# Keys of batches five to eight transposed by VectorE and DMA instead of TensorE, in a pooled-attention and expert kernel

## The chip, the core and the metric

The kernel runs on one core of one Trainium2 chip. A core has TensorE (PE, the matrix engine; its weight loads are listed as PEld), VectorE (DVE), ScalarE (ACT), GpSimd (POOL), the sync engine (SP), whose queue issues nearly all DMAs here, and 16 DMA engines. The metric is device time in microseconds (us) of one execution. Three executions of the kernel before gave 905.93, 906.12 and 907.04 us; the median is 906.12 us.

## What is computed

Two steps follow each other. The first is attention against pooled keys and values, for 8 batches, 8 heads, 576 positions and a head size of 64. The second is an expert layer with a sine in it, on 4608 tokens.

```python
k_p = k.reshape(B, H, Sp, pool, D).mean(axis=3)      # pool = 8, Sp = 72
v_p = v.reshape(B, H, Sp, pool, D).mean(axis=3)
scores = scale * np.matmul(q, k_p.transpose(0, 1, 3, 2))
scores = scores - np.max(scores, axis=-1, keepdims=True)
attn = np.exp(scores)
attn = attn / (np.sum(attn, axis=-1, keepdims=True) + 1e-09)
x = np.matmul(attn, v_p)                  # then (4608, 512)
h = x @ w_in
s = np.sin(alpha * h)
g = h + s * s / (alpha + 1e-09)
out = g @ w_out
```

Everything is float32. Of each head there are 72 pooled keys, each a sum over 8 neighbouring positions (the division by 8 is folded into the scale of the exponential).

## The kernel before

The work is written out by hand, in an order that each engine keeps: an instruction that waits holds up all that come behind it on its engine. The first expert product runs in nine units of 512 tokens. A unit has 28 slots, 4 groups (`J`) of 7 (`k`); in a slot TensorE does one product of the expert layer (`product`, line 837, four matmuls at line 845, each of them two records in the trace). The products follow a Strassen scheme, so VectorE and ScalarE form sums and copies between them. `carry(u)` (line 1175) puts the other work into the slots of unit u: `at(slot, f, ...)` appends f to the work of a slot. In units 1 to 6 this is the attention of batch b = u + 1, hidden beside the products, and the preparation of batch b + 1. (Batches are counted from 0 in the code, so "five to eight" are 4 to 7.) After the ninth unit, from about 430 us on, the second expert product runs; the change does not touch it.

The way of the keys of one batch:

- `load_k` (line 116) loads half of the heads in one DMA on SP's queue, 576 KB into the tile `kvin` (two buffers, shared with the values). A partition holds 24 consecutive positions, that is 3 pooled keys, of one head; 4 heads of 24 such rows make 96 partitions, head by head.
- `pool_rows` (line 127) adds the 8 positions on POOL, in three additions (line 131), the last of which writes half of the tile `kp` of 96 x (3 keys x 128). There is one buffer of `kp`.
- `k_t` (line 273) turns `kp` with three TensorE transposes (line 278) into a PSUM bank, and VectorE copies the bank to `kblk` (line 279), 64 rows of one half of the heads over 64 of the other, the 72 keys of a head in their natural order. There are two tiles `kblk`, for even and odd batches.
- `two_scores` (line 303) multiplies the turned queries, as weights, with the 72 key columns of each head (line 317): 72 matmuls of 64 x 64 x 72 per batch, in two blocks, each 72 columns side by side in a PSUM bank. `shifts` (line 328) subtracts the maximum on VectorE, and `exp`, `norm`, `turn` and `move` follow: `turn` (line 495) transposes in blocks of 32 x 32 on VectorE, `move` (line 514) puts the blocks to their places with 16 DMAs on SP's queue (line 521). `all_values` (line 600) ends the batch.

In unit u with 0 < u < 7, before the change: `sums_of_x` (line 806, VectorE, line 814) for products 7 and 4 in slot 0; scores in slots 3 and 5; `load_v` in slot 6; `load_q` of batch u + 2 in slot 7; `load_k` of batch b + 1 and its pooling in slot 12; `move` in slot 14; the queries of batch u + 2 are turned on VectorE and moved by 16 DMAs (`turn_q`, line 215, DMAs at line 243) in slots 23 to 25; `all_values` in slot 25; `k_t` of batch b + 1 in slot 26. In slot 2 VectorE also finishes the last group of the unit before (`finish`, line 1051, additions at line 1052), which frees a PSUM bank that the scores of slot 3 write. `store_g` (line 1063, DMAs at line 1066) stores a group's result.

Of the kernel before, what the change touches and what calls it, by code (L numbers as in the profile page):

```python
# [13 lines left out]
F32 = mybir.dt.float32  # L14
# [6 lines left out]
POOL = 8  # L21
# [19 lines left out]
class Kernel:  # L41
# [74 lines left out]
    def load_k(self, b, e):  # L116

        Sp, D, NP = self.Sp, self.D, self.NP
        m = Sp // 3
        t = self.kvp.tile([P, 2048], F32, name="kvin")[:NP * m, 0:3 * POOL * D]  # L120
        self.nc.sync.dma_start(out=t, in_=self.k[b, NP * e:NP * e + NP].rearrange("h (p x) d -> (h p) (x d)", x=3 * POOL))
# [136 lines left out]
    def attention(self, b):  # L258
# [14 lines left out]
        def k_t():  # L273
# [5 lines left out]
            nc.vector.tensor_copy(out=kb[:].rearrange("p hp (x j) -> p j hp x", j=3), in_=ps.rearrange("p j (hp x) -> p j hp x", hp=NP))  # L279

        def q_t(i, copy=nc.scalar.copy):

            n = rows[i]
# [19 lines left out]
        def two_scores(j):  # L303
# [3 lines left out]
            for i, banks in ((2 * j, (x, 7)), (2 * j + 1, (5, 6))):  # L307
# [3 lines left out]
                for t in (i, 4) if i == 3 else (i,):  # L311
                    for hp in range(NP):
                        r0, h = (64 * (hp // 2), NP + hp % 2) if t == 4 else (0, hp)
                        for r, q in columns(hp, t):
                            for e in range(2):
                                s = slice(64 * e, 64 * e + 64)
                                nc.tensor.matmul(ps[e][r0 + r:r0 + r + q.shape[-1], h, :], q[s], kb[s, hp, :], start=True, stop=True)  # L317
            for i, m, ps in tiles:
# [281 lines left out]
        def all_values():  # L600
# [30 lines left out]
        return SimpleNamespace(**{f.__name__: f for f in (k_t, q_t, products, score, two_scores, two_shifts, exp, norm, new_a, turn, move, values, values_rest, all_values,  # L631
                                                          k_head, k_last, q_head, rest_q, products_head, soft_shift, soft_exp, norm_head, norm_rest, a_head, a_rest)})
# [542 lines left out]
    def carry(self, u):  # L1175
# [57 lines left out]
        if 0 < u < last:  # L1233
# [367 lines left out]
```

## Time and profile before

| | |
|---|---|
| median of three runs | 906.12 us |
| profiled execution, device time | 903.92 us |
| its span, first to last instruction | 902.1 us |
| PE busy | 894.4 us (99%) |
| DVE busy | 679.4 us (75%) |
| ACT busy | 448.6 us (50%) |
| POOL busy | 212.2 us (24%) |
| granted TensorE clock | 1.00 |
| one unit of 1 to 5 (for instance 195 to 250 us) | 55 us: DVE busy 37.8, ACT 41.1, POOL 25.5; DMA engines 0.71 of the time |

The span is the time from the first to the last instruction of the profiled execution; some 1.8 us more lie around it. TensorE is busy nearly always, so a change in time has to appear as work that TensorE no longer does, or does more slowly, or as a wait in front of it. In a row of the timeline stand start, length, engine, line and operation of a run of like instructions, and in brackets how long the engine was idle before it and what ended that. The rows of one engine can overlap a little, since consecutive instructions are pipelined.

### The profile page before, as it was taken

What the parts mean: (1) busy time and instruction counts of PE and PEld (TensorE: products, weight loads), DVE (VectorE), ACT (ScalarE), POOL (GpSimd) and SP (SyncE); (2) the same over time, 40 slices, a digit from 0 to 9 for tenths busy, and PEclk for the clock granted to TensorE, in tenths of its full rate; (3) what the DMA queues carried; (4) which work ended last, traced back from release to release, by engine and by line L of the source; (5) the groups of instructions that cost most, each with busy time, mean ns of one, the idle gap of its engine ahead of it and who ended that gap; (6) DMA issues with size and microseconds to landing.
All of it is one profiled execution on the core that took longest, in us unless ns stands there. A gap on an engine that the chain in (4) does not pass through costs nothing.

```text
span 902.1 us, 17919 instructions
## 1 busy us (share of the span) xinstructions
PE 894.4 (99%) x7002; PEld 815.4 (90%) x7002; DVE 679.4 (75%) x1012; ACT 448.6 (50%) x1072; POOL 212.2 (24%) x216
## 2 busy tenths in 40 slices
PE   9999999999999999999999999999999999999998
PEld 5787888888888888888888999999999999999997
DVE  7685867768577675764558799979798888889895
ACT  5686776877768777687976611211111111111111
POOL 5797452824337252430000000000000000000000
PEclk9999999999999999999999999999999999999999
DMA  9955857759486595658226346261618162533401
GB/s 260 249 182 171 232 154 203 190 167 260 136 215 185 181 225 145 173 148 292 93 75 224 101 144 198 59 195 37 224 28 230 33 196 68 172 92 125 139 14 40
DMA packets 128746, 141.12 MB, mean 156 GB/s; under 512 B 46920, under 2 KB 95704, under 8 KB 128664
## 3 DMA queue, kind: packets, MB, share of 16 engines
q1 hardware_dynamic: 125880, 137.88, 53.4%
q10 hardware_dynamic: 2784, 2.11, 0.9%
q8 instruction: 55, 0.90, 0.5%
q14 instruction: 27, 0.22, 0.1%
HBM read 75.37 MB, written 47.19 MB: 136 GB/s over the span
## 4 chain that ended last, share of the span: by engine, by line
PE 96%; DVE 2%; ACT 1%; issue 0%; ACTq 0%; DVEq 0%
PE PS L845 44%; PE PS L1334 41%; PE PS L1030 3%; PE PS L317 2%; PE PS L610 2%; PE PS L623 1%; DVE x L1289 1%; PE PS L1098 0%; DVE s L1289 0%; ACT s L1007 0%; PE PS L422 0%; DVE h L1052 0%; DVE r L1289 0%; PE PS L568 0%; PE PS L289 0%; PE PS L278 0%
## 5 line engine op out<-in xcount | busy, mean ns | idle before, releaser
L845 PE MATMUL PS<-home,a 128*128 128x256 f32 x1104 | 258.0, 381 | 0.7 <-DVE h L819 0.6
L845 PEld LDWEIGHTS PS<-home,a 128*128 128x128 f32 x1104 | 205.3, 190 | 33.1 <-issue 4.5
L845 PE MATMUL PS<-home,as 128*128 128x256 f32 x768 | 182.7, 382 | 0.0
L845 PEld LDWEIGHTS PS<-home,as 128*128 128x128 f32 x768 | 141.8, 190 | 19.7 <-ACT PS L820 1.2
L1384 POOL TENSOR_TENSOR cc<-cc,cb 128x576 f32<-128x576 f32 x1 | 2.0, 1978 | 501.6 <-DVE cb L1289 501.6
L1334 PE MATMUL PS<-s,wb 128*128 128x144 f32 x896 | 119.1, 286 | 0.0
L1334 PEld LDWEIGHTS PS<-s,wb 128*128 128x128 f32 x896 | 113.7, 190 | 0.1
L1007 ACT ACTIVATE s<-s,c 128x256 f32<-128x256 f32 (+1 forms) x228 | 113.5, 565 | 0.0
L819 DVE TENSOR_TENSOR h<-PS,p 128x512 f32<-128x512 f32 x72 | 49.1, 683 | 62.9 <-PE PS L845 37.3
L131 POOL TENSOR_TENSOR kvin<-kvin 96x768 f32<-96x768 f32 (+3 forms) x42 | 74.2, 1768 | 72.2 <-DMA kvin<-in_v_dram 70.0
L1462 ACT COPY PS<-PS 128x144 f32<-128x144 f32 x56 | 14.7, 263 | 144.8 <-PE PS L1334 140.7
L1000 ACT ACTIVATE s<-h,al 128x256 f32<-128x256 f32 x144 | 65.6, 509 | 37.3 <-DVE h L819 37.3
L1334 PE MATMUL PS<-r,wb 128*128 128x144 f32 x512 | 73.3, 286 | 0.3 <-DVE r L1289 0.3
L1334 PE MATMUL PS<-s,a 128*128 128x144 f32 x512 | 73.2, 286 | 0.0
L1000 ACT ACTIVATE s<-PS,al 128x256 f32<-128x256 f32 x144 | 60.0, 469 | 20.2 <-PE PS L845 19.2
L1052 DVE TENSOR_TENSOR h<-PS,s 128x512 f32<-128x512 f32 x36 | 24.7, 686 | 58.5 <-ACT s L1007 58.5
L1334 PEld LDWEIGHTS PS<-r,wb 128*128 128x128 f32 x512 | 67.1, 190 | 0.5 <-DVE r L1289 0.5
L1334 PEld LDWEIGHTS PS<-s,a 128*128 128x128 f32 x512 | 67.0, 190 | 0.0
L820 ACT COPY PS<-PS 128x512 f32<-128x512 f32 x72 | 41.5, 576 | 35.6 <-PE PS L845 30.8
L1482 ACT COPY PS<-PS 128x144 f32<-128x144 f32 x56 | 14.7, 263 | 88.1 <-PE PS L1334 88.1
L1052 DVE TENSOR_TENSOR h<-h,s 128x1024 f32<-128x1024 f32 x36 | 55.3, 1537 | 0.9 <-ACT s L1007 0.9
L1334 PE MATMUL PS<-s,we 128*128 128x144 f32 x384 | 54.9, 286 | 0.0
(216 smaller groups left out, 1407.6 us busy)
## 6 DMA issues: line engine op xcount, KB each, us to landing
g_bridge<-h SPq DMA_DIRECT2D x72, 512.0 KB
r<-g_bridge SPq DMA_DIRECT2D x31, 1152.0 KB
out_dram<-o SPq DMA_DIRECT2D x122, 72.0 KB
kvin<-in_k_dram SPq DMA_DIRECT2D x14, 576.0 KB
q<-in_q_dram SPq DMA_DIRECT2D x7, 1024.0 KB
kvin<-in_v_dram SPq DMA_DIRECT2D x14, 512.0 KB
aM<-tr SPq DMA_DIRECT2D x54, 92.0 KB
aM<-tr SPq DMA_DIRECT2D x54, 88.0 KB
```

The lines of the kernel that those rows point to most:

```text
L131: self.nc.gpsimd.tensor_tensor(out=t[..., 0:w] if w > D else out, in0=t[..., 0:w], in1=t[..., w:2 * w], op=OP.add)
L317: nc.tensor.matmul(ps[e][r0 + r:r0 + r + q.shape[-1], h, :], q[s], kb[s, hp, :], start=True, stop=True)
L610: nc.tensor.matmul(o[r:r + 64], w, x, start=start and i < 2, stop=False, skip_group_check=True)
L819: add = lambda o, x, y: nc.vector.tensor_tensor(out=o, in0=x, in1=y, op=OP.add)
L820: copy = lambda o, x: nc.scalar.copy(out=o, in_=x)
L845: nc.tensor.matmul(ps[:, jj, :], self.A[p][:, kk, f * P:(f + 1) * P], x[:, kk, :], start=(start and n == 0), stop=(kk == 1), skip_group_ch ...
L1000: self.nc.scalar.activation(out=G.s[:, i, jj, j, :], in_=src[:, jj], func=AF.Sin, scale=self.al[:, f:f + 1])
L1007: self.nc.scalar.activation(out=x, in_=x, func=AF.Square, scale=self.c[:, f:f + 1])
L1030: nc.tensor.matmul(o, W[m][:, G.J - J0], X[m], start=start and n == 0, stop=True, skip_group_check=True)
L1052: add = lambda o, x, y: self.nc.vector.tensor_tensor(out=o, in0=x, in1=y, op=OP.add)
L1334: nc.tensor.matmul(out, W[:, J // 2, J % 2, :], A[:, J, :], start=(start and J == 0), stop=(J == self.NJ - 1), skip_group_check=True)
L1462: nc.scalar.copy(out=x1[:, 0, :], in_=x0[:, 1, :])
```

## The change

For batches 4 to 7 the keys are turned another way. The rows of `load_k` stand in another order: the 4 heads of the same 24 positions next to each other (partition = 4 x group + head). `k_turn` transposes `kp` (96 x 384) in blocks of 32 x 32 in one VectorE instruction into a new tile `k_tr`. `k_move` then copies 12 pieces of 32 partitions x 96 elements (384 bytes per partition, contiguous on both sides) from `k_tr` into `kblk` with 12 DMAs on SP's queue. The keys of a head then lie in `kblk` in three runs of 24, in an order in which the third of a key's index comes first; the score matmuls read these three runs and write each result column to the natural place of its key, so that within a run neighbouring columns are written in steps of three elements (12 bytes) of PSUM. The softmax behind it sees the same layout as before.

The places: the keys of batch 4 are loaded in slot 22 and pooled in slot 27 of unit 1, those of batches 5, 6 and 7 in slot 12 of units 2, 3 and 4 (before: in slot 12 of the units 2, 3, 4 and 5 for batches 4 to 7). `k_turn` stands in slot 0, behind the two `sums_of_x`, and `k_move` in slot 8, of the unit before the batch's own (units 2 to 5). `k_t` in slot 26 is left in units 0 and 1 only. Batches 1 to 3 go the old way.

```diff
 load_k:
-        self.nc.sync.dma_start(out=t, in_=self.k[b, NP * e:NP * e + NP].rearrange("h (p x) d -> (h p) (x d)", x=3 * POOL))
+        src = self.k[b, NP * e:NP * e + NP].rearrange("h (p x) d -> h p (x d)", x=3 * POOL)
+        self.nc.sync.dma_start(out=t, in_=src.rearrange("h p x -> (h p) x" if b < 4 else "h p x -> p h x"))
 attention:
+        def k_turn():
+            kp = self.kp.pop(b)
+            self.k_tr = self.ap.tile([NP * Sp // 3, 4 * NP * Sp // 3], F32, name="k_tr")[:]
+            nc.vector.transpose(out=self.k_tr.rearrange("p (c h j x) -> p j c x h", c=4, h=NP, j=3),
+                                in_=kp[:].rearrange("p j e d -> p j (e d)").rearrange("p j (c x h) -> p j c x h", c=4, h=NP))
+        def k_move():
+            n = NP * Sp // 3
+            for c in range(4):
+                for a in range(3):
+                    nc.sync.dma_start(out=kb[32 * c:32 * c + 32].rearrange("p h x -> p (h x)")[:, n * a:n * a + n],
+                                      in_=self.k_tr[32 * a:32 * a + 32, n * c:n * c + n])
+        def keys(hp, s, out):
+            if b < 4:
+                return out, kb[s, hp, :]
+            w = Sp // 3
+            k = kb[s].rearrange("p h x -> p (h x)").rearrange("p (a n) -> p a n", a=3)[:, :, w * hp:w * hp + w]
+            return out.rearrange("p (a x j) -> p a j x", a=3, j=3), k.rearrange("p a (j x) -> p a j x", j=3)
 two_scores:
-                                nc.tensor.matmul(ps[e][r0 + r:r0 + r + q.shape[-1], h, :], q[s], kb[s, hp, :], start=True, stop=True)
+                                out, k = keys(hp, s, ps[e][r0 + r:r0 + r + q.shape[-1], h, :])
+                                nc.tensor.matmul(out, q[s], k, start=True, stop=True)
 carry:
             for i in range(2):
-                if b < last:
-                    at(12, self.load_k, b + 1, i)
+                ahead = b + 1 + (u > 1)
+                if ahead <= last:
+                    at(12, self.load_k, ahead, i)
                     at(12, lambda i=i: self.pool_k[i]())
+                if u == 1:
+                    at(22, self.load_k, b + 2, i)
+                    at(27, lambda i=i: self.pool_k[i]())
             at(25, A.all_values)
-            if b < last:
+            if u == 1:
                 at(26, self.att[b + 1].k_t)
+            elif b < last:
+                at(0, self.att[b + 1].k_turn)
+                at(8, self.att[b + 1].k_move)
```

More of the change, by code (lines that the diff above doesn't have):

```diff
@@ L629, in all_values @@
             to_x(rest, slice(0, 4), 512, 64)
[L631 removed]
+        return SimpleNamespace(**{f.__name__: f for f in (k_t, k_turn, k_move, q_t, products, score, two_scores, two_shifts, exp, norm, new_a, turn, move, values, values_rest, all_values,
                                                           k_head, k_last, q_head, rest_q, products_head, soft_shift, soft_exp, norm_head, norm_rest, a_head, a_rest)})
```

## The prediction

> **What bounds the kernel now.** I read the page's first part and its chain first. PE is busy for all but some 8 us of the span, and the chain that ended last is PE's for 96%; lines 317 (scores, 2%) and 278 (the transposes that go, 0%) both lie on it.
>
> ```profile
> PE 894.4 (99%) x7002; PEld 815.4 (90%) x7002; DVE 679.4 (75%) x1012; ACT 448.6 (50%) x1072; POOL 212.2 (24%) x216
> ...
> PE 96%; DVE 2%; ACT 1%; issue 0%; ACTq 0%; DVEq 0%
> ```
>
> So only three things count: what TensorE no longer does, what it does more slowly, and new waits ahead of it. Next I read the timeline of unit 3, around slot 26 (the transposes), slots 0 to 3 (where VectorE gets the new work) and the scores:
>
> ```profile
> 190.56 2.00 PE L845 MATMUL PS<-home,a 128*128 128x256 f32 x8
> ...
> 192.39 0.41 PE L278 MATMUL PS<-ident,kp 96*128 96x96 f32 x3
> ...
> 192.64 1.92 PE L845 MATMUL PS<-home,as 128*128 128x256 f32 x8
> ...
> 193.25 0.55 DVE L279 COPY kblk<-PS 128x288 f32<-128x288 f32 x1
> ...
> 198.53 0.94 DVE L814 TENSOR_TENSOR home<-home,home 128x512 f32<-128x512 f32 x1
> ...
> 200.69 0.69 DVE L1052 TENSOR_TENSOR h<-PS,s 128x512 f32<-128x512 f32 x1 [1.23 <-ACT s L1007]
> ...
> 201.44 1.18 PEld L317 LDWEIGHTS PS<-kblk,q 64*64 64x64 f32 x64 [0.38 <-DVE h L1052]
> 201.44 1.33 PE L317 MATMUL PS<-kblk,q 64*64 64x72 f32 x64
> ```
>
> To see here: the first transpose starts at 192.39 and the next product at 192.64, so the three hold TensorE for 0.25 us, about 83 ns each; the 0.41 is with the pipeline's tail. VectorE ends its slot 0 at 199.47 and then stands idle for 1.23 us until ScalarE's squares are done; its next addition frees the bank for which TensorE waits 0.38 us. That is the place to watch, since `k_turn` comes between the two. The idle time is the same 1.23 us in units 2, 4 and 5 (before the additions at 145.63, 255.95 and 311.01).
>
> Then SP's queue in the same unit, past slot 8, and from the chain in order of time two blocks of line 610 and the two score blocks of unit 1:
>
> ```profile
> 209.18 2.68 SPq L105 DMA_DIRECT2D q<-in_q_dram  x2
> 217.10 0.90 SPq L1066 DMA_DIRECT2D g_bridge<-h  x2
> 218.10 2.12 SPq L121 DMA_DIRECT2D kvin<-in_k_dram  x2
> 226.99 10.81 SPq L521 DMA_DIRECT2D aM<-tr  x16
> ```
>
> ```profile
> 78.62 2.33 PE PS L610 x43
> ...
> 91.33 1.30 PE PS L317 x62
> ...
> 96.29 1.46 PE PS L317 x78
> ...
> 132.15 2.33 PE PS L610 x43
> ```
>
> SP stands idle from 211.86 to 217.10 and from 220.2 to 227.0. One batch's scores take 1.30 + 1.46 = 2.76 us of TensorE.
>
> **The parts of the change.**
>
> *Transposes removed (TensorE).* Four batches x 3 x 83 ns = 4 x 0.25 = 1.0 us, all on the path. Around them the trace shows 0.7 us more of "issue" idle time in two places over the seven batches, one of 0.37 us in unit 3 at 247.59; whether it belongs to the transposes is not shown. Ends: a gain of 1.0 to 1.7 us. I take 1.0. The copy at line 279 (0.55 us of VectorE each) goes too, but behind it VectorE is idle for 0.8 us waiting for TensorE, so it is worth nothing.
>
> *k_turn (VectorE, slot 0 of units 2 to 5).* Transposes of 128x512 take 0.687 us (line 501) and of 128x256 0.402 us (line 508): 1.11 ns an element, so 384 elements come to 0.54 us. Its output is scattered in steps of 96 bytes, which no transpose of the trace has. The nearest row is the copy at line 279, which writes in steps of 12 bytes: 0.549 us, against 0.447 us of a reduction of the same 288 elements (line 340), 23% more. So 0.54 to 0.66 us, and if POOL works beside it perhaps as much longer as line 814 gets (0.69 to 0.94 us, 37%): 0.9 us. Even twice the plain time, 1.08 us, fits into the idle 1.23 us. Cost 0; without that cover every 0.1 us beyond would reach the scores through the wait of line 317, four times. Upper end, at three times the plain time: 4 x 0.4 = 1.6 us.
>
> *Batch 4's earlier load (unit 1).* SP is free at 129.45, and the DMA engines are 16% busy from 132 to 135 us, so the 1.15 MB should land by about 136 us (stretches of this window reach 380 GB/s). The pooling took 7.9 us in unit 2 (171.94 to 179.87), and its third addition must wait for the transposes at 137.5 anyway: done at about 143 to 144 us. VectorE reaches `k_turn` at 144.4, or 144.9 if POOL slows two more of its sums; its next addition is due at 145.63. So it fits by some 0.2 us. Queued behind it: the bank for the scores. Cost 0; upper end 1.5 us, once, if the load lands that much later. POOL's own next work there, the sums at line 804, starts one or two us later and is covered, as POOL is idle until the values land at 158.77. Unit 5 loses its load and pooling, for which nothing waited: no gain.
>
> *k_move (SP, slot 8).* 12 issues at the 0.59 us median of lines 521 and 243 are 7.1 us. In unit 3 they would run from 211.86 to 218.9, so the store and the load of slots 10 and 12 come 1.8 us later; in the other units 0.4 to 1.5 us. All is caught up in the idle time before the moves at 226.99. The stored buffer is wanted again only two groups later, the loaded keys only in the next unit, and the moved keys land some 40 us before their scores. Its 384 packets are small against the 128746 of the page. Cost 0. The keys' other row order in `load_k` moves the same bytes in the same 6 KB rows; at worst it lands a little later, and is covered in the same way.
>
> *Waits ahead of the scores.* The keys are now written by 12 DMAs and not one copy. TensorE's queue spends 51 ns on each semaphore; line 317 has 49 of them in 7 batches and already waits for queries that DMAs wrote later than these. Line 610, fed by 16 DMAs, shows 3.4 us of "issue" in 7 batches, 0.49 each. So 0 to 4 x 0.49 = 2.0 us; I take 0, as the row of the same line with its DMA-fed weights is the nearest.
>
> *The scores themselves.* They read three runs of 24 columns and write PSUM in steps of 12 bytes. For the reading there is a row: line 610 reads runs of 32 elements in another order for batch 1 (the block at 78.62) and whole rows for batch 2 (132.15), and both take 2.33 us, so it costs nothing. For the writing there is none: every matmul here writes neighbouring columns. Lower end 0, as a gain is excluded: the columns are as many. Upper end, a column at half speed: 4 x 2.76 = 11.0 us. For 0 speak the reading row, and the slow column rate: a 256-column record takes 228 ns of TensorE (the chain has 16 in 3.65 us), 0.89 ns a column. ScalarE reads PSUM in steps of 512 bytes (line 537, 128x512: 0.595 us) as fast as neighbouring columns (line 820: 0.576 us). Against it speaks the 23% of line 279, for writes to SBUF. The rows of reads are two, and I take 0, but not firmly.
>
> The Trainium skill speaks against that step. Its page "SBUF — State Buffer", in the section "Door 1: The DMA port swizzle", says that PSUM has lines of 8 bytes, two float32 values, and that any non-contiguous access pattern there slows matmuls significantly. No run here shows it yet. By that rule the sum would end in a loss of several us; by the rows it ends in the gain of 1.0.
>
> **Sum.** −1.0 + 0 = −1.0 us. The profiled execution took 903.92 us (902.1 of span and 1.8 around it), so it would become 902.9. The median of the runs is 906.12, 2.2 us above the profiled one; I carry the difference over: 905.1 us.
>
> **The rivals.**
>
> 1. *The step of 12 bytes slows the scores* (other side). Place: line 317 of batches 4 to 7, in slots 3 and 5 of units 3 to 6. At half speed +11.0 − 1.0 = 916 us; at 1.5 times the time +5.5 − 1.0 = 910.6. From 9% on (0.25 of 2.76 us) it eats the gain, from 25% (0.70 us) the kernel is slower by over 0.2%. For it: no row of such writes, and the SBUF row with 23%. Against it: the rows of strided reads. Chance 0.30.
> 2. *New waits eat the gain*: semaphores in front of the scores (2.0 us) or late pooling before unit 2 (1.5 us). Half of both is 1.75 us, so +0.75 in all: 906.9 us. For it: the "issue" gaps of line 610 and only 0.2 us of spare time in unit 2. Against it: the DMAs of the queries are waited for already. Chance 0.10.
> 3. *More goes than the three transposes*: the 0.44 us over which their weight loads stretch (192.17 to 192.61) in each of the four units, and the 0.37 us in unit 3, 4 x 0.44 + 0.37 = 2.1 us: 904.0 us. For it: weight loads fill 90% of the span. Against it: the starts at 192.39 and 192.64 lie 0.25 apart. Chance 0.13.
>
> **How the numbers follow.** The forecast has the remaining 0.47, with a range of its own of 904.2 to 906.2 us. About 0.2%, 1.8 us, is what a measurement of this kernel can tell from no change; the forecast of −1.0 lies inside. Within 0.2%: nearly all of the forecast (0.42) and half of rival 2 (0.05), 0.47. Slower: rival 1 and the rest of rival 2, 0.35. Faster: rival 3 and what of the forecast reaches beyond 1.8 us (0.05), 0.18. The range of 903.9 to 911.0 leaves out the upper half of rival 1 (0.14) and a little below.
>
> **What would show it.** Right: line 278 has 9 transposes and line 279 three copies; the score blocks of units 3 to 6 keep 1.30 and 1.46 us; a transpose of 0.54 to 0.66 us stands in VectorE's idle time of units 2 to 5, and line 1052 behind it still waits for ScalarE; the wait of line 317 stays at 0.38 us; a unit of 2 to 5 is 0.25 us shorter. Wrong: score blocks above 1.6 us (rival 1); line 1052 waiting for POOL or DMA, or a wait of line 317 above 0.5 us (rival 2).

## The result, and the profile after

The change made the kernel slower: 927.02 us (median of six executions, 924.56 to 929.47) against 906.02 us for six of the kernel before (903.88 to 907.04), a ratio of 1.0233 with a 95% interval of 1.0215 to 1.0250. I had forecast 905.1 us, in a range of 903.9 to 911.0. The profiled execution of the kernel after took 928.09 us with a span of 926.3 us, 24.2 us more than the span of before.

In the kernel after, the lines below the new functions have moved: the products are line 870 (before 845), the scores 342 (317), the moves of the softmax blocks 546 (521), the stores of a group 1091 (1066), VectorE's last additions 1077 (1052), the key load 122 (121), `all_values` 635 and 648 (610 and 623). `k_turn` is line 286, `k_move` line 294. Some experiments shift them by up to four lines.

From the page of the kernel after: busy time, the clock in 40 slices, and the chain that ended last by engine.

```profile
PE 905.1 (98%) x6990; PEld 817.4 (88%) x6990; DVE 676.8 (73%) x1012; ACT 448.8 (48%) x1072; POOL 209.7 (23%) x216
...
PEclk9999999989989899999999999999999999999999
...
PE 72%; DMA 11%; SPq 5%; DVE 4%; POOL 4%; issue 1%; ACT 1%; ACTq 0%; POOLq 0%; DVEq 0%
```

TensorE has twelve matmul records less and is busy 10.7 us longer. The chain, 96% TensorE before, now passes through DMAs and SP's queue for 16%, and three slices of the clock row are below 9. To find the place I took the starts of the first score block of each unit, which are 55.06 to 55.26 us apart before:

| first score block to the next, us | unit 1 to 2 | 2 to 3 | 3 to 4 | 4 to 5 | 5 to 6 |
|---|---|---|---|---|---|
| before | 55.06 | 55.07 | 55.26 | 55.06 | 55.06 |
| after | 55.95 | 62.27 | 62.38 | 63.51 | 54.78 |

The units 2, 3 and 4 lose 7.20, 7.12 and 8.45 us, together 22.8; the late pooling of batch 4 costs 0.89 us; unit 5 is 0.28 us shorter. The remaining 0.8 us lie ahead of the first score block of unit 1, where the change does nothing. Unit 5 tells most: it has all of the new work but one thing. It turns and moves the keys of batch 7 and scores those of batch 6 in the new way, but loads no keys any more.

The parts that I had feared do not show. The timeline of the kernel after, unit 3 (start, length, engine, line, and in brackets the idle time ahead):

```profile
207.38 0.94 DVE L839 TENSOR_TENSOR home<-home,home 128x512 f32<-128x512 f32 x1
208.25 0.85 DVE L286 STREAM_TRANSPOSE k_tr<-kp 96x384 f32<-96x384 f32 x1
209.55 0.69 DVE L1077 TENSOR_TENSOR h<-PS,s 128x512 f32<-128x512 f32 x1 [0.45 <-ACT s L1032]
210.30 1.33 PE L342 MATMUL PS<-kblk,q 64*64 64x72 f32 x64
...
255.05 1.25 DVE L229 STREAM_TRANSPOSE tr<-q 128x1024 f32<-128x1024 f32 x1 [6.48 <-DMA aM<-tr]
...
255.17 2.23 PE L635 MATMUL PS<-aM,vm 64*64 64x512 f32 x8 [4.03 <-DMA aM<-tr]
```

`k_turn` fits into VectorE's idle time, and the addition behind it still waits 0.45 us for ScalarE. The first score block takes 1.33 us as before. The last row is the loss: 45 us later TensorE waits 4.03 us for the moved softmax blocks, ahead of `all_values`. Before, the same line (610) began without a wait, 40.8 us behind the score block; now it begins 44.9 us behind it. Its row in the kernel before:

```profile
242.21 0.65 PE L610 MATMUL PS<-aM,vm 64*64 64x512 f32 x6
```

VectorE waits for the same moves: its turn of the next queries (line 229) writes the buffer that they still read. The addition that stands behind that turn (line 1077, at 256.22) frees a PSUM bank of `all_values`, so late moves can hold up TensorE a second time.

The groups of the scores in the two kernels are the same to the nanosecond (226 ns mean, 19.9 us in all). The first row is from the kernel before, the other two from the kernel after, the last is `k_turn` (busy us, mean ns):

```profile
L317 PE MATMUL PS<-kblk,q 64*64 64x72 f32 x1008 | 19.9, 226 | 0.0
...
L342 PE MATMUL PS<-kblk,q 64*64 64x72 f32 x1008 | 19.9, 226 | 0.8 <-DVE h L1077 0.8
L286 DVE STREAM_TRANSPOSE k_tr<-kp 96x384 f32<-96x384 f32 x4 | 3.4, 857 | 0.0
```

SP's queue in unit 3 of the kernel after, past slot 8 (start, time from the first issue of the row to its last, issues):

```profile
222.03 12.20 SPq L294 DMA_DIRECT2D kblk<-k_tr  x12
...
235.47 2.14 SPq L122 DMA_DIRECT2D kvin<-in_k_dram  x2
237.70 15.75 SPq L546 DMA_DIRECT2D aM<-tr  x16
```

Before, the key load was issued 16.7 us behind the first score block of the unit, SP then stood idle for 6.8 us, and the sixteen moves took 10.81 us, from 25.5 to 36.4 us behind that block. Now the twelve new moves take 12.20 us and not 7.1, the key load goes out at 25.2 us, the softmax blocks' moves follow right behind it, from 27.4 to 43.1 us, and take 15.75 us. What SP waits for, in the kernel after (us in total, times, longest):

```profile
SPq L546 <- DMA kvin<-in_k_dram: 15.2, 6, 3.7
SPq L294 <- DMA q<-in_q_dram: 11.9, 4, 3.3
SPq L294 <- DMA kvin<-in_v_dram: 7.5, 4, 2.2
SPq L294 <- DMA vr<-in_v_dram: 2.7, 6, 0.9
```

None of these waits is one of data: the moves of the keys do not need the queries or the values, and the softmax blocks' moves do not need the keys. They have another reason. Each DMA of the trace carries one of eight completion semaphores, used in turn (numbers 100, 102 and 104 to 109). The table has some DMAs of unit 3 with their issue, semaphore, number of increments and landing:

```
issue    sem  incr. landed           what
215.13.. 105-108    223.57 224.60 225.69 226.64   four loads of values (vr)
223.59   105  16    230.67  (+7.08)  k_move 2
224.62   106  16    230.86  (+6.24)  k_move 3
225.70   107  16    231.04  (+5.34)  k_move 4
226.66   108  16    231.22  (+4.57)  k_move 5
235.47   100  13    244.19  (+8.72)  key load 1
236.46   102  13    247.31  (+10.85) key load 2
237.70   104  16    247.62  (+9.91)  softmax blocks 1
240.87   109  16    249.11  (+8.24)  softmax blocks 6
244.20   100  16    250.38  (+6.18)  softmax blocks 7
247.32   102  16    250.62  (+3.29)  softmax blocks 8
252.87   102  16    254.97  (+2.10)  softmax blocks 16
```

A DMA is issued 0.01 to 0.02 us after the one eight places before it has landed, and not earlier: `k_move` 2 to 5 behind the four loads of values (223.57 to 226.64), the seventh and eighth move of softmax blocks behind the two key loads. So one queue has eight DMAs in the air at most. Before, SP issued its moves into a nearly empty queue: in unit 3 they landed 2.1 us after their issue (the last four 2.9 to 4.0), three or four in the air, and the limit held up none of them. It did stand in the trace of before, in the opening: between 28.8 and 37.9 us SP issued twelve loads, each 0.02 to 0.06 us after the landing eight places before. Two of the waits of SP that this made there (loads of weights and of values, behind loads of weights that they do not need):

```profile
SPq L679 <- DMA a<-in_moe_w_in_dram: 1.1, 3, 0.4
...
SPq L145 <- DMA a<-in_moe_w_in_dram: 1.1, 2, 0.9
```

The table has a second effect: a small DMA issued right behind the key load lands with it (+9.91, +8.24 us), and alone after 2.1 us.

Last, TensorE around its wait, in windows of 2 us of the kernel after (busy us of each engine, then the granted clock, the DMA engines' share and GB/s):

```profile
250.00:252.00 2.00, 1.14 (x8) 0.86 (x6) 0.00 (x0) 2.00 (x6) 1.25 (x2) 1.00 0.59 142
252.00:254.00 2.00, 0.00 (x0) 0.00 (x0) 0.00 (x0) 0.25 (x1) 0.00 (x0) 0.93 0.59 139
254.00:256.00 2.00, 0.83 (x2) 0.32 (x4) 0.95 (x1) 0.00 (x0) 0.00 (x0) 0.50 0.89 304
256.00:258.00 2.00, 2.00 (x24) 1.08 (x24) 2.00 (x4) 0.00 (x0) 0.00 (x0) 0.50 0.71 265
258.00:260.00 2.00, 2.00 (x24) 1.05 (x20) 1.71 (x3) 0.90 (x3) 0.00 (x0) 0.50 0.10 25
260.00:262.00 2.00, 2.00 (x22) 0.57 (x14) 0.00 (x0) 0.00 (x0) 0.00 (x0) 0.86 0.57 136
```

The last matmul ends at 251.14, the clock falls to 0.50 at about 253.7, TensorE starts again at 255.17, and the full clock is back at about 260.6. It works 5.4 us at half speed, which loses 2.7 us: 4.03 + 2.7 = 6.7 us. The unit is 7.4 us longer than its 55.26 less the 0.28 that unit 5 gained. The other 0.7 us are not the clock's: in the run with the load on more engines (below), at a clock of 1.00, TensorE is also busy for 55.91 us of unit 3, where it is for 54.78 in unit 5 here; why is not shown. In each of the units 2, 3 and 4 the clock stands at 0.50 for 6.83 us. This is also why TensorE counts as busier after the change: I estimate from these stretches that about 9 of the 10.7 us more are slow matmuls.

### The profile page after: what moved, and what is told of

It reads as the page before. It is cut to its first block, busy times and chain, and to the rows that moved or that the text cites. A ratio compares the mean times of both kernels' runs of the same rounds, so it can differ in the third digit from the quotient of the medians.

```text
span 926.3 us, 17931 instructions
## 1 busy us (share of the span) xinstructions
PE 905.1 (98%) x6990; PEld 817.4 (88%) x6990; DVE 676.8 (73%) x1012; ACT 448.8 (48%) x1072; POOL 209.7 (23%) x216
## 4 chain that ended last, share of the span: by engine, by line
PE 72%; DMA 11%; SPq 5%; DVE 4%; POOL 4%; issue 1%; ACT 1%; ACTq 0%; POOLq 0%; DVEq 0%
PE PS L1366 40%; PE PS L870 26%; DMA kvin<-in_k_dram 5%; DMA kvin<-in_v_dram 3%; SPq L546 2%; PE PS L635 2%; DMA q<-in_q_dram 2%; POOL kvin L132 1%; PE PS L1055 1%; SPq L704 1%; DVE h L1077 1%; PE PS L342 1%; PE PS L648 1%; DMA a<-in_moe_w_in_dram 1%; DMA aM<-tr 1%
## 5 line engine op out<-in xcount | busy, mean ns | idle before, releaser
L132 POOL TENSOR_TENSOR kvin<-kvin 96x768 f32<-96x768 f32 (+3 forms) x42 | 70.7, 1684 | 106.9 <-DMA kvin<-in_v_dram 69.3
L1025 ACT ACTIVATE s<-h,al 128x256 f32<-128x256 f32 x144 | 65.6, 509 | 36.4 <-DVE h L844 36.4
L1366 PE MATMUL PS<-x,wb 128*128 128x144 f32 x384 | 54.9, 286 | 0.0
```

The source lines that it names most:

```text
L132: self.nc.gpsimd.tensor_tensor(out=t[..., 0:w] if w > D else out, in0=t[..., 0:w], in1=t[..., w:2 * w], op=OP.add)
L1025: self.nc.scalar.activation(out=G.s[:, i, jj, j, :], in_=src[:, jj], func=AF.Sin, scale=self.al[:, f:f + 1])
L1366: nc.tensor.matmul(out, W[:, J // 2, J % 2, :], A[:, J, :], start=(start and J == 0), stop=(J == self.NJ - 1), skip_group_check=True)
```

## The experiments

The theory after the first look: the twelve moves on SP's queue push the late-landing key loads in front of the softmax blocks' moves, TensorE waits for these, and the clock doubles the price. The rivals: the new row order of the load, the moves' bytes on the DMA engines, the length of SP's own work, and the new place of `k_turn`. All ratios are against the kernel before, run on the same chip beside the experiment; the unit times are from the profiled executions, and where a median and its profiled execution lie some us apart the text says so.

### The row order alone, in the kernel before

```diff
-        ... in_=self.k[b, NP * e:NP * e + NP].rearrange("h (p x) d -> (h p) (x d)", x=3 * POOL)
+        ... in_=...rearrange("h (p x) d -> h p (x d)", x=3 * POOL).rearrange("h p x -> p h x") if b > 3 else (as before)
```

> The kernel before, with only the row order of the key loads of batches 4 to 7 changed (the keys then stand in a wrong order; the work is the same). Theory Queue: 906 us, as before. Theory Load: slower by several us, 910 to 927. Theory Both: the load lands 3 to 4 us later, partly behind the first moves, which are issued 7 us after it: 906 to 909 us. In all of them the load's time to landing and the packets tell whether it runs on fewer engines: the page should then count 32 packets under 512 bytes fewer.

Measured: 905.00 us against 905.14, 1.0003 (0.9993 to 1.0013); all units 55.06 to 55.25. The new order costs nothing by itself where the load is early, as theory Queue had it. It is slower in most units, though: its two DMAs land 6.5 to 8.5 and 7.4 to 10.1 us after their issue (in units 2 to 4 of the kernel after 7.8 to 9.0 and 10.8 to 11.1), before 6.3 to 7.4 and 7.4 to 8.1, and they count 13 increments and not 16. The profile has 32 packets less, 4 for each of the eight loads. Both fit a load on 12 DMA engines and not 16. The Trainium skill, on its page "DMA: Bandwidth & Descriptors" in the section "Why a DMA increments its semaphore by 16 and not by 1", says that a DMA uses the largest number of engines up to 16 that divides the slowest dimensions of both sides, and that the issuing sequencer adds the missing increments at once; here these are 24 groups on one side and 96 partitions on the other, so 12 engines, and 12 increments and one for the rest make the 13 of the trace.

### The kernel after with the old row order

```diff
-        self.nc.sync.dma_start(out=t, in_=src.rearrange("h p x -> (h p) x" if b < 4 else "h p x -> p h x"))
+        self.nc.sync.dma_start(out=t, in_=src.rearrange("h p x -> (h p) x"))
```

> The changed kernel, but all key loads in the old row order (head by head); the keys of batches 4 to 7 then land in wrong places, the work is the same. Theory Queue (the 12 small moves push the loads and the moves behind them on SP's queue): still 920 to 927 us. Theory Load (the new row order lands late, 10 to 11 us after issue, and the rest follows): about 905 us. Theory Both (SP's queue lets only a few DMAs be under way, so a late load directly ahead of the 16 moves holds them): moves no longer wait for the key load, but start some 2 us later than before, 905 to 909 us.

Measured: 912.34 us against 905.14, 1.0079 (1.0059 to 1.0100); units of 55.18, 59.14, 56.86, 58.88 and 54.78. So nearly 15 of the 21 us hang on the row order, though alone it costs nothing: in unit 3 the two key loads land after 6.5 and 8.0 us, SP's waits for them in front of line 546 fall from 15.2 to 9.7 us, and the last move of unit 3 lands 40.9 us behind the score block (after 44.7, before 38.0). What is left is a third of the loss, without any of the new row order; theory Both came nearest and was too low. TensorE waits for the moved blocks here too, though its own row calls the break "issue": it ends at 188.55 us, 0.20 us after the last of them landed (188.35). In the kernel after, where the row names them, the distance is the same (254.97 and 255.17). VectorE's row names them here, and the second break of TensorE stands behind that:

```profile
188.53 1.25 DVE L229 STREAM_TRANSPOSE tr<-q 128x1024 f32<-128x1024 f32 x1 [3.31 <-DMA aM<-tr]
...
188.55 1.08 PE L635 MATMUL PS<-aM,vm 64*64 64x512 f32 x4 [0.77 <-issue]
...
189.70 0.65 DVE L1077 TENSOR_TENSOR h<-PS,s 128x512 f32<-128x512 f32 x1
...
190.41 0.33 PE L635 MATMUL PS<-aM,vm 64*64 64x64 f32 x4 [0.78 <-DVE h L1077]
```

So the cause is that of the kernel after, with shorter waits, and still the clock falls. The windows of unit 2:

```profile
188.00:190.00 2.00, 1.08 (x4) 0.22 (x4) 1.47 (x2) 0.90 (x2) 0.00 (x0) 1.00 1.00 375
190.00:192.00 2.00, 1.59 (x24) 1.12 (x28) 2.00 (x3) 0.70 (x3) 0.00 (x0) 0.69 0.44 158
192.00:194.00 2.00, 2.00 (x26) 1.01 (x18) 1.19 (x2) 0.20 (x1) 0.00 (x0) 0.50 0.26 61
```

TensorE has two breaks of 0.8 us here, with four matmuls between them, and is idle for a third of the 4 us from 188 on. That was enough for the half clock.

### The kernel after without the twelve moves

```diff
-                at(8, self.att[b + 1].k_move)
```

> The changed kernel without the 12 moves (the scores of batches 4 to 7 then use older keys). Theory Queue: about 905 us, a gain of 1 against the kernel before. Theory Load: still above 920 us. Theory Both: the key load is issued some 8 us ahead of the moves again and has landed by then but for 2 us: 905 to 908 us.

Measured: 905.38 us against 905.14, 1.0001 (0.9991 to 1.0010). The units are 56.63, 54.78, 54.79, 54.78 and 54.78. With the moves gone the key load goes out early again, 17 us behind the score block, and the slower row order is harmless: the loss of units 2 to 4 needs the moves. All other parts of the change are worth 0.28 us a unit (0.47 in the one of 55.26), and the first unit loses 1.57 us.

### The load on more engines

```diff
+            for g in (slice(0, 16), slice(16, m)):
+                self.nc.sync.dma_start(out=t[NP * g.start:NP * g.stop], in_=src[:, g].rearrange("h p x -> p h x"))
```

> The changed kernel, moves in slot 8 as changed, but each key load of batches 4 to 7 in two DMAs, 64 and 32 partitions (16 groups of 4 heads and 8). If the new row order is slow because its DMA runs on 12 of the 16 engines, two thirds of the bytes are back on 16, and the load lands 1 to 2 us sooner: 914 to 922 us, between the old rows (912.3) and the change (927). If it is slow because of the order in which the rows are read, nothing is gained and SP has two issues more: 927 us or more.

Measured: 916.89 us against 905.46, 1.0120 (1.0086 to 1.0154); the profiled execution was a shorter one (913.34 us, units of 55.33, 57.31, 57.40, 58.13 and 54.78). In units 2 to 4 the parts land 5.4 to 7.2 us after their issue, SP waits 5.6 us for key loads in front of the moves, and TensorE 2.7 us for the moved blocks. A load that lands 4 us sooner gives back about half of the loss, with two DMAs more on the queue, inside the range that I had for fewer engines. In the profiled execution the clock stayed at 1.00, though TensorE had pairs of breaks here too (0.7 and 0.8 us in unit 3, 1.5 and 0.7 in unit 4).

### The twelve moves behind the softmax blocks' moves

```diff
-                at(8, self.att[b + 1].k_move)
+                at(20, self.att[b + 1].k_move)
```

> The changed kernel with the 12 small moves in slot 20 instead of slot 8, so behind the stores and moves of the attention and ahead of the queries' moves; all else as changed, with the new row order. Theory Lanes (a DMA of this queue waits until the one eight before it has landed; what lies behind the big loads waits for them): in slot 20 nothing big is under way, so the units 2 to 5 take 54.8 to 55.2 us again, and only the late pooling ahead of unit 2 is left: 905 to 906.5 us. Rival (the 12 moves cost SP's time, 7 us a unit, wherever they stand, and now delay the queries' moves by 3 us): scores of units 3 to 6 wait for queries, 908 us or more.

Measured: 914.72 us against 905.46, 1.0102 (1.0079 to 1.0126), units of 55.27, 55.60, 57.22, 57.34 and 57.91. This missed my expectation. Line 635 no longer waits, as expected, but the twelve issues now push the stores of a group, whose buffer VectorE wants back, and the queries' moves. The waits of this kernel:

```profile
DVE h L844 <- DMA g_bridge<-h: 12.4, 4, 3.2
DVE tr L526 <- DMA g_bridge<-h: 6.8, 3, 2.7
```

And the same with `k_turn` in slot 7 in place of slot 0:

```diff
-                at(0, self.att[b + 1].k_turn)
-                at(8, self.att[b + 1].k_move)
+                at(7, self.att[b + 1].k_turn)
+                at(20, self.att[b + 1].k_move)
```

> As the run with the moves in slot 20, and the turn on VectorE in slot 7 instead of slot 0, so that batch 4's late pooling has 14 us more. Theory Lanes, and the gain of the transposes as predicted (0.28 to 0.47 us in each of four units, 1.3 us): 903.5 to 904.5 us, faster than the kernel before by 0.1 to 0.15%. Rival: as in the other run, 908 us or more.

Measured: 917.69 us against 905.46, 1.0128 (1.0108 to 1.0149), units of 55.07, 55.48, 58.41, 57.35 and 58.08; VectorE waits 15.0 us for the stores. A miss as well: `k_turn` was not what cost there, though the first unit, at 55.07, shows no late pooling any more. In slot 20 SP has no free 7 to 12 us either; who is pushed depends on the slot.

### The moves on another queue

```diff
-                    nc.sync.dma_start(out=kb[32 * c:32 * c + 32]...
+                    nc.gpsimd.dma_start(out=kb[32 * c:32 * c + 32]...
-                at(8, self.att[b + 1].k_move)
+                at(3, self.att[b + 1].k_move)
```

> The changed kernel with the 12 small moves issued by POOL in slot 3, while POOL waits for the values, instead of by SP in slot 8. Theory Lanes: SP's queue stands as without the moves, units 2 to 5 at 54.8 us, unless POOL takes over 0.9 us for one issue and so holds the pooling of the values and the norms: 905 to 907 us. Rival (the DMA engines, not the queue, are what is short ahead of the moves): 912 us or more, as the same bytes are moved at the same time as the loads.

Measured: 907.34 us against 905.46, 1.0021 (1.0004 to 1.0038), units of 55.82, 55.98, 55.10, 55.10 and 55.10. The same bytes from another queue cost nearly nothing in this slot, and so again in the next run in slot 18. So the moves' bytes on the DMA engines and the landing of the keys are not what costs; no run has them on POOL in slot 8. POOL's rows of unit 3 show the limit of eight a second time, on a queue of its own (issues, and in brackets what it waited for):

```profile
205.86 3.97 POOL L294 DMA_DIRECT2D kblk<-k_tr  x8
210.39 0.50 POOL L294 DMA_DIRECT2D kblk<-k_tr  x1 [0.56 <-DMA kblk<-k_tr]
211.99 0.99 POOL L294 DMA_DIRECT2D kblk<-k_tr  x2 [1.10 <-DMA kblk<-k_tr]
214.63 0.50 POOL L294 DMA_DIRECT2D kblk<-k_tr  x1 [1.66 <-DMA kblk<-k_tr]
```

Eight are issued in a row, 0.5 us each; behind them POOL issues as the landings eight places before allow. The 0.3 us by which a unit is longer here than without the moves (55.10 against 54.78) have a row too: line 342 counts 73 semaphores and not 49, 6 more for each of four batches, at 51 ns.

```diff
-                at(0, self.att[b + 1].k_turn)
-                at(8, self.att[b + 1].k_move)
+                at(7, self.att[b + 1].k_turn)
+                at(18, self.att[b + 1].k_move)          # and k_move issued by POOL, as above
```

> The kernel after with the twelve moves issued by POOL in slot 18 and the transpose of the keys on VectorE in slot 7 in place of slot 0; nothing of the computation is left out. Theory (only the moves' stand on SP's queue costs, beside 0.3 us per batch for the 24 semaphores that TensorE counts more ahead of the scores): units of 55.1 us as with the moves on POOL in slot 3 (55.10), and no late first unit, since the transpose no longer waits for the pooling of batch 4 (there 0.8 us): 905.0 to 906.2 us, within 0.1% of the kernel before. Rival (the moves cost wherever they are issued, through the DMA engines): over 907 us, with waits of TensorE for the moved softmax blocks in front of line 635. If the semaphores go with the later slot, 904 us.

Measured: 906.56 us against 905.52, 1.0008 (0.9998 to 1.0018), units of 55.06, 54.78, 55.11, 55.10 and 55.10. The units are as the theory had them, the first one included; the median lies 0.4 us above its range. The waits of line 635 are gone, and the extra semaphores stay (3.1 us in place of 2.3):

```profile
PEld PS L635 <- issue: 3.4, 15, 0.3
PEld PS L342 <- issue: 3.1, 11, 0.3
```

This is the best complete form of the change that I found, and it is no faster than the kernel before.

### The key loads behind the softmax blocks' moves

```diff
-                ahead = b + 1 + (u > 1)
-                if ahead <= last:
-                    at(12, self.load_k, ahead, i)
-                    at(12, lambda i=i: self.pool_k[i]())
                 if u == 1:
+                    at(12, self.load_k, b + 1, i)
+                    at(12, lambda i=i: self.pool_k[i]())
+                if b + 2 <= last:
                     at(22, self.load_k, b + 2, i)
                     at(27, lambda i=i: self.pool_k[i]())
```

> The changed kernel, with the keys of batches 5 to 7 loaded in slot 22 and pooled in slot 27 of units 2 to 4, as batch 4's are in unit 1; nothing else moved. Theory Queue and theory Both: the moves of slot 14 have no load directly ahead of them any more, so the 7 to 8 us a unit go; what is left is the 0.9 us a unit that unit 1 to 2 shows (late pooling before slot 0): 905.9 - 1.0 + 4 x 0.9, about 908 us. Theory Load: the late landing only moves elsewhere, above 912 us.

Measured: 909.80 us against 905.14, 1.0050 (1.0033 to 1.0067), units of 56.32, 56.43, 56.80, 57.19 and 56.29. The profiled execution took 912.15 us. TensorE no longer waits for the moved blocks, as theory Queue and theory Both had it; its weight loads wait 8.5 us for VectorE in front of the scores, more than they left for that. Then with `k_turn` moved to slot 7:

```diff
-                at(0, self.att[b + 1].k_turn)
+                at(7, self.att[b + 1].k_turn)
```

> The kernel after with the key loads of batches 5 to 7 in slot 22 and their pooling in slot 27, as in the run with late loads, and the transpose of the keys in slot 7 in place of slot 0; the twelve moves stay on SP in slot 8. Nothing of the computation is left out. With late loads nothing late stands in front of the softmax blocks' moves, and TensorE did not wait for them. Theory (what was left of the loss there was the transpose in slot 0, waiting for the late pooling and holding up the addition that frees the bank of the scores): no wait of TensorE for the moved blocks, units of 54.8 to 55.5 us, 904.5 to 907 us, so the twelve moves on SP would cost nothing once no key load stands between them and the softmax blocks' moves. Rival (the pooling itself, running on POOL beside VectorE's sums of slot 0, which took 2.2 us in place of 0.9, holds up the scores): units over 56 us, 908.5 to 911 us.

Measured: 911.36 us against 905.41, 1.0066 (1.0053 to 1.0080); the profiled execution took 909.44 us, with units of 55.12, 56.84, 56.64, 56.48 and 55.02. The theory missed and the rival holds, with a median 0.4 us above its range: the late pooling beside VectorE's sums costs units 2 to 4 some 1.4 to 1.8 us each, and 1.4 to 2.1 with `k_turn` in slot 0. But the question for which it was run has its answer in SP's rows:

```profile
218.60 11.09 SPq L294 DMA_DIRECT2D kblk<-k_tr  x12
...
231.44 11.07 SPq L546 DMA_DIRECT2D aM<-tr  x16
...
243.78 2.14 SPq L122 DMA_DIRECT2D kvin<-in_k_dram  x2
```

The twelve moves take 11.09 us here too, waiting for the landings of queries and values. The moves behind them take 11.07 us and not 15.75, end 38.3 us behind the score block (204.24), and TensorE waits for none of them. The pooling side, VectorE and POOL in the same kernel one unit later:

```profile
256.01 3.66 POOL L132 TENSOR_TENSOR kvin<-kvin 96x768 f32<-96x768 f32 x2
...
256.52 2.30 DVE L839 TENSOR_TENSOR home<-home 128x512 f32<-128x512 f32 x1
258.74 1.48 DVE L839 TENSOR_TENSOR home<-home,home 128x512 f32<-128x512 f32 x1
...
260.88 1.35 PE L342 MATMUL PS<-kblk,q 64*64 64x72 f32 x64 [0.83 <-DVE h L1077]
```

A sum of 0.95 us takes 2.30 us while POOL adds beside it, and the scores wait. The first unit of the kernel after has the same: `k_turn` (at 146.61 us) did not wait there for batch 4's pooling, which had ended at 145.27, but for the four sums beside it, which took 4.7 us in place of 3.2 before.

### The key loads on another queue

```diff
+        queue = self.nc.gpsimd if b > 4 else self.nc.sync
-        self.nc.sync.dma_start(out=t, in_=src.rearrange(...))
+        queue.dma_start(out=t, in_=src.rearrange(...))
```

> The kernel after with one edit: the key loads of batches 5 to 7 are issued by POOL and not by SP, in the same slot; the twelve moves stay on SP in slot 8. Nothing of the computation is left out. Theory 'landings' (SP issues a DMA only when the one eight before it has landed, and the softmax blocks' moves stand right behind the late key loads): the moves of the keys still take 10 to 12 us of SP, but nothing late is left in front of the softmax blocks' moves, so these land at 38 to 41 us after the unit's first score block (before: 38.0, after: 44.6), TensorE waits at most 1 us for them and its clock stays at 1.00; units 2 to 4 take 54.8 to 55.8 us and the kernel 905 to 908.5 us. Rival 'SP's own time' (twelve issues of 0.6 us and their waits push the softmax blocks' moves too far, whoever issues the loads): units 2 to 4 over 58 us, 915 us or more.

Measured: 916.93 us against 905.52, 1.0138 (1.0101 to 1.0175); the profiled execution took 915.37 us, with units of 56.75, 56.15, 62.19, 55.45 and 54.78. The result lies between the theories. Two of the three units are within about 1.1 us of before, but unit 3 has the whole loss again:

```profile
248.45 1.07 PE L636 MATMUL PS<-aM,vm 64*64 64x512 f32 x4 [2.30 <-DMA aM<-tr]
250.51 0.48 PE L636 MATMUL PS<-aM,vm 64*64 64x64 f32 x4 [0.98 <-DVE h L1078]
```

There the second key load was issued by POOL at 242.33, and the last two moves of softmax blocks, issued by SP at 242.38 and 243.01, landed 5.4 and 5.3 us later, with it (248.08), while those just before landed in 2.2. So the queue is only a part of it: a small DMA that starts behind a large load lands with it, even when another queue issued that.

### Waits of TensorE made in the kernel before

```diff
-                at((12, 13, 13, 13)[i], A.turn, i)
-            at(14, A.move, range(4))
+                at((12, 13, 13, 17)[i], A.turn, i)
+            at(17, A.move, range(4))
```

> The kernel before with the last of the four turns of the softmax blocks in slot 17 and not 13, and their sixteen moves behind it in slot 17; nothing of the change is in it, and nothing of the computation is left out. By the rows of before the turn then ends some 8 us later (235 and not 227 us in unit 3), the last move lands at about 247.5 us, and line 610, due at 242.2, waits about 5 us, in each of the six units. Theory 'clock' (a wait of 4 us or more halves TensorE's clock from about 3 us after its last matmul to about 6 us after it starts again, which costs some 3 us more): units of 62 to 64 us, the granted clock 0.50 around each wait, the kernel 945 to 962 us. Rival 'only the wait' (the halved clock seen in the kernel after belongs to something else of the change): units of 60.0 to 60.8 us at a clock of 1.00, 930 to 940 us.

```diff
-            at(14, A.move, range(4))
+            at(14, A.move, range(1))
+            at(18, A.move, range(1, 4))
```

> The kernel before with twelve of the sixteen moves of the softmax blocks in slot 18, behind the store of slot 17, and four in slot 14 as before; nothing of the change is in it, and nothing of the computation is left out. By the rows of before the store is ready at 233.4 us, so the last move is issued at about 241.5 and lands at about 243.8: line 610, due at 242.2, waits 1 to 2 us in each of the six units. Theory 'clock' (only a wait of some 3 us or more takes the clock down): units longer by the wait itself, 56 to 57.3 us, the clock 1.00 throughout, 911 to 920 us. Rival (every wait in front of line 610 costs about twice its length): units of 57.5 to 59 us and a clock below 1.00, 920 to 930 us.

Measured: 960.95 us against 905.41, 1.0617 (1.0601 to 1.0633), units of 64.17 to 65.13; and 940.92 us, 1.0393 (1.0379 to 1.0407), units of 61.56 to 63.17. The first total is that of theory 'clock', with units a little longer; the second lies above both of its ranges. The waits of line 610 in the first, then in the second kernel (total, times, longest):

```profile
PE PS L610 <- DMA aM<-tr: 26.4, 6, 5.2
```

```profile
PE PS L610 <- DMA aM<-tr: 16.1, 6, 3.2
```

The second kernel's waits came out at 1.8 to 3.2 us and not 1 to 2: the store in front of the twelve moves was ready when I had read (32.0 us behind the score block), but the first moves behind it took 0.9 to 1.6 us each to issue in place of 0.6. Of its six waits, the one of 1.76 us, in unit 6, left the clock at 1.00, and the five of 2.4 to 3.2 us did not. Windows of the second kernel, where the wait runs from 256.9 to 260.2:

```profile
258.00:260.00 2.00, 0.00 (x0) 0.00 (x0) 0.00 (x0) 0.04 (x1) 0.00 (x0) 0.80 0.51 118
260.00:262.00 2.00, 1.83 (x6) 0.39 (x8) 1.95 (x3) 0.00 (x0) 0.00 (x0) 0.50 0.00 0
262.00:264.00 2.00, 2.00 (x26) 1.45 (x28) 2.00 (x3) 0.90 (x3) 0.00 (x0) 0.50 0.00 0
264.00:266.00 2.00, 2.00 (x24) 0.87 (x16) 0.71 (x1) 0.00 (x0) 0.00 (x0) 0.50 0.42 98
```

With nothing of the change in the kernel, waits of 2.4 to 3.2 us come with units 6.5 to 8.1 us longer, and waits of 3.9 to 5.2 us with units 9.1 to 9.9 us longer, that is 3.4 to 5.5 us beyond the wait; small breaks beside the wait are in that. The half clock belongs to the wait. Each stretch of it lasts 6.83 us, or 3.41 (two of the five in the second kernel, one of the six in the first). The Trainium skill describes it on its page "TensorE: Matmul & The Clock Gate", in the section "HAM oscillation — how this bites in real kernels", as half speed after an idle gap of more than about 3.4 us; the trace agrees on the half speed (0.50), but shorter gaps were enough: 2.4 to 3.2 us here, and two breaks of 0.8 us in the kernel with the old row order.

### What the change would be worth

```diff
-                at(0, self.att[b + 1].k_turn)
-                at(8, self.att[b + 1].k_move)
+                at(7, self.att[b + 1].k_turn)
```

> The kernel after without its twelve moves, and with the transpose of the keys in slot 7; the scores of batches 4 to 7 use the keys that an older batch left in the tile, so the moves are left out of the time. It measures what the change is worth when nothing has to be moved. Theory: units 2 to 5 at 54.78 us as without the moves before, against 55.06, and now the first of them too, which lost 1.57 us to the late pooling of batch 4: 904.0 to 904.6 us, 0.1% faster than the kernel before; the upper end of my first estimate for the three transposes and what lies around them, 1.7 us, would give 903.7. Rival (the late pooling of batch 4 was not what lengthened that unit): 905.4 us as without the moves and with the transpose in slot 0.

Measured: 904.91 us against 905.52, 0.9990 (0.9982 to 0.9999), units of 55.22, 55.66, 54.78, 54.78 and 54.79. The first unit shows what `k_turn` in slot 0, behind the sums that the late pooling slows, had cost there; 0.40 us of the second unit's 0.88 are a wait of a product for VectorE, the rest I did not trace. Even with nothing to move, the gain is 0.6 us in the medians, 0.28 us in an undisturbed unit.

## Why the prediction was wrong

*The step that failed* is "k_move (SP, slot 8)", with its last words: "All is caught up in the idle time before the moves at 226.99 ... Cost 0." Three of its terms were wrong. (Its 384 packets, too, are the rows of one batch; the page of the kernel after counts 2273 packets more in all.)

- Its length. I took twelve issues at 0.59 us, 7.1 us. Measured were 10.6 to 12.2 us, since SP issues a DMA only when the one eight places before it has landed, and the eight before the moves were loads of values and queries that take 8 to 12 us. The rate of 0.59 us came from rows in which DMAs of 2 us followed each other. The limit of eight could have been read in the opening of the trace of before.
- Its cover. The idle time of SP was there, but what it had covered was the key load's flight. Pushed 8.5 us later, that load stood right ahead of the softmax blocks' moves, which then waited for it twice over: in the queue (15.2 us of SP) and on the DMA engines (8 to 10 us to land in place of 2.1). The last moved block came 6.7 us later in the unit, where 2.8 us were to spare.
- The next to be late. I had named the stored buffer, the loaded keys and the moved keys as those who wait for these DMAs. The moves of line 521, whose reader is TensorE, were missing, though the step names them as the end of the idle time; so was VectorE's turn of the queries, which waits for them too. And a wait of 4 us of TensorE cost the unit 7 us, of which the half clock made 2.7.

*Also mis-sized:* the keys' other row order "at worst lands a little later": it was up to 3 us for the load, free where there is room, and nearly 15 of the 21 us where there is none. Batch 4's earlier load: forecast 0 with 1.5 at most, and the unit lost 0.89 us. The term that was too small there is POOL's effect on VectorE: the sums beside the pooling took up to 1.4 us each, and 2.2 in the kernel without the twelve moves, where I had 0.94.

*Right:* the transposes, 4 x 0.25 = 1.0 us, measured 0.28 us in an undisturbed unit and 0.48 in unit 3. `k_turn`, at 0.857 us above the plain 0.54 to 0.66 us but inside the 0.9 that I had with POOL beside it, and hidden in the idle time of units 3 to 5. No new wait ahead of the scores from the semaphores. And the step of 12 bytes in PSUM, on which the largest rival stood: 226 ns a matmul before and after. There the rows of strided reads were the better guide; the sentence of the Trainium skill's page "SBUF — State Buffer" ("Door 1: The DMA port swizzle"), that any non-contiguous access pattern in PSUM slows matmuls significantly, does not hold for these float32 matmuls of 64 x 64 x 72.

*The rivals:* the direction that I gave 0.35 came true, but by none of them. Rival 2, new waits, had the right kind and the wrong place: it looked in front of the scores, not of `all_values`. Rival 1 falls with the 226 ns, and rival 3 with the gain of 0.28 us a unit, where it had 0.44.

Left open is how much of the row order's share comes through SP's queue and how much through the DMA engines; the loads on POOL's queue show only that both take part. How short a break of TensorE leaves the clock alone is narrowed but open: past the opening of the programs, single waits up to 1.8 us left it in all runs, waits from 2.1 us on took it down, and pairs of breaks of 0.6 to 1.5 us did either.

## What to carry to other kernels

Idle time of a queue is not free room: ask what is in flight during it, and what the DMAs behind it will share the engines with. A move of DMAs is priced with the queue's eight landings and not with the issue rate, and the question behind it is always whose data stand next in that queue. Where TensorE is busy all the time, price a wait of 2.4 us or more at its length and 3.4 to 5.5 us on top, as the waits of these runs cost.

## What the runs showed of the hardware that I had not expected

- At most eight DMAs of one queue are in flight in this program, with its eight completion semaphores to a queue: on SP (`k_move` issued 0.02 us after the landing eight places before) and on POOL (eight issues in 3.97 us, then as the landings allow).
- A small DMA behind a large load lands with it, 8 to 10 us after its issue in place of 2.1, and also when another queue issued the load (5.4 us).
- A load whose slowest dimension is 24 took 7.4 to 11.1 us for its second DMA in place of 7.4 to 8.1 before, with 13 increments and 4 packets less.
- TensorE's clock fell to 0.50 some 1.9 to 5.3 us after a wait had begun, which could be after its end, and stayed there for 6.83 or 3.41 us each time.
- Float32 matmuls that write PSUM in steps of 12 bytes were as fast as with neighbouring columns.
